# A two-layer expert network on one core: four products of each up-projection burst share one PSUM bank, with three additions in place of five

## The chip, the cores and the metric

The kernel runs on one core of a Trainium2 chip. The metric is the time of one execution in device microseconds; before the change it is 1911.4 us, the median of three runs (1910.29 to 1911.5). The core has five engines that run beside one another and wait for one another by semaphores: TensorE (PE in the profile, its weight loads PEld), VectorE (DVE), ScalarE (ACT), GpSimd (POOL) and SyncE (SP), which here only issues transfers. Each engine takes its instructions in the order in which they stand in its own program.

## The reference

Three parts follow one another. A linear attention over 4 batches of 576 rows gives 2304 rows of 512 numbers. A mixture of 8 experts, all of them applied to every row and weighted by a probability that a Sinkhorn iteration makes, follows; then a feed-forward layer.

```python
h = np.maximum(x @ w1[e], 0.0)            # 2304x512 @ 512x1024, for each e of 8
out += P[:, e:e + 1] * (h @ w2[e])        # 2304x1024 @ 1024x512
...
h = x @ w_in                              # 2304x512 @ 512x2048
g = h * np.clip(h + 3.0, 0.0, 6.0) / 6.0
return g @ w_out
```

## The kernel before

Inputs are float32. Each operand of a large product is split into a float16 high part and a float16 rest, and a product is three matmuls: high by high, high by rest, rest by high.

The up-projection (`x @ w1`) goes by Winograd's form of Strassen's scheme: rows and columns are cut into halves, and seven products of quarter size take the place of eight. For that, seven operands of x lie ready in `xbuf` (QB11, QB21, QB22, QT4, QT1, QT2, QT3 in this order, made by `combine_steps` or `forms`), and seven of a weight slice in `w1buf` (QA11, QA12, QS4, QA22, QS1, QS2, QS3, made by `w1_steps`). The index in `prod(bank, i, first, last)` picks the pair.

The work is cut into 20 slices of 512 hidden columns (`s`, 16 for the experts, 4 for the feed-forward layer) and three pairs of row groups (`p`). `step(s, p, prev)` calls `up_burst` twice, each on a quarter of the slice (`qf` 0 and 1). A burst has seven products of six matmuls of 384 columns (L905), which land in four PSUM banks A, B, C and D of the pool `ps_u`. Two products that belong to one sum are accumulated into one bank by TensorE; the other sums are made by `add` (L913) on VectorE, which reads a bank, scales it and adds an SBUF tile. ScalarE copies bank A out twice (L944 and L951). `emit` then makes the two float16 parts of a hidden tile `h` from a finished sum: ScalarE applies the activation (L933, L937, in the feed-forward layer L927) and the cast (L934, L929), VectorE or GpSimd forms the rest (L935, L938, L930), and in the feed-forward layer VectorE also does L928.

Between the products stand three down-projection tiles of the step before (`down_tile`, L978: twelve matmuls of 512 columns into one of two banks `y`), which VectorE adds onto `acc` (L988). `between[0]` to `between[2]` are these three calls.

All other work is cut into small steps that wait in queues: `tick()`, called at the end of each product and twice in each down tile, takes the next one from `ticks`, `side` or `back`. In `side` lie the scaling and splitting of the next weights (L207 on ScalarE, L208 on VectorE, L269 on GpSimd); in `back` the conversion of the float64 weights of the last layer (L324 to L345, of which L345 is ScalarE's); in `ticks` the rest of the attention, the gate, and the making of the feed-forward layer's x (`x2_steps`, L1022 and L1023, then L377, L378, L382).

There are 60 steps. Steps 6 to 44 and 50 to 59 stand under `tc.manual_schedule()`: there each engine's order is that of the code. The first six steps, and steps 45 to 49, in which the last expert slices and the first feed-forward slice meet `x2_steps`, are ordered by the scheduler of the framework. In the first two of these (s 0 and the p 1 step of s 0) there are no down tiles between the products.

Of the kernel before, what the change touches and what calls it, by code (L numbers as in the profile page):

```python
# [9 lines left out]
F32 = mybir.dt.float32  # L10
# [3 lines left out]
AF = mybir.ActivationFunctionType  # L14
ALU = mybir.AluOpType
# [16 lines left out]
QB11, QB21, QB22, QT4, QT1, QT2, QT3 = range(7)  # L32
# [3 lines left out]
H_DOWN = 2.0 ** -20  # L36
# [4 lines left out]
def tile_attention_moe_ffn(  # L41
# [12 lines left out]
    nc = tc.nc  # L54
    B, H, S, D = q.shape
    NT, DM = out.shape
    E, _, F = w1.shape
    P = 128
# [4 lines left out]
    GN = GJ * P  # L63
# [13 lines left out]
    ps_u = ctx.enter_context(tc.tile_pool(name="ps_u", bufs=1, space=bass.MemoryType.PSUM))  # L77
# [24 lines left out]
    def rt(name):  # L102
        return rpool.tile([P, GN], F32, tag="r", name=name)
# [264 lines left out]
    def combine_steps(p, cp, bs):  # L368


        b11, b21, b12, b22, t1, t2 = bs
        dst = xop[p]
        V, G = nc.vector, nc.gpsimd

        def sp(qd, src, eng):
            def f():
                nc.scalar.copy(dst[:, qd, 0, cp], src)  # L377
                eng.tensor_sub(dst[:, qd, 1, cp], src, dst[:, qd, 0, cp])  # L378
            return f

        def tt(o, a, b):
            return lambda: V.tensor_sub(o, a, b)  # L382

        return [
            tt(t1, b12, b11),
            lambda: (tt(t2, b22, t1)(), sp(QB11, b11, V)()),
            lambda: (sp(QT2, t2, G)(), tt(b12, b22, b12)()),
            lambda: (sp(QT1, t1, V)(), sp(QB21, b21, G)()),
            lambda: (tt(t1, t2, b21)(), sp(QT3, b12, V)()),
            lambda: (sp(QT4, t1, V)(), sp(QB22, b22, G)()),  # L390
        ]

# [9 lines left out]
    def attention(pr):  # L402
# [207 lines left out]
        def forms(p, cp, bank):  # L610

            ga, gb = PAIRS[p]
            dst = xop[p]
            ps = {}

            def out_(ps_, qd):
                nc.scalar.copy(dst[:, qd, 0, cp], ps_)
                nc.vector.tensor_tensor(out=dst[:, qd, 1, cp], in0=ps_, in1=dst[:, qd, 0, cp], op=ALU.subtract)

            def onto(ps_, qds):  # L620
                for m, qd in qds:
                    for hl in range(2):
                        nc.tensor.matmul(
                            ps_, m, dst[:, qd, hl, cp], start=False, stop=True, skip_group_check=True
                        )

            def plain(c, g, qd):
                def f():
                    ps[qd] = bank(f"f{p}_{cp}_{qd}")
                    xset(ps[qd], c, g)  # L630
                    out_(ps[qd], qd)
                return f

            def f_t1():
                b = bank(f"f{p}_{cp}_t1")
                xset(b, cp, gb)
                onto(b, [(minus, QB11)])
                out_(b, QT1)

            def f_on(qd, qds):  # L640
                def f():
                    onto(ps[QB22], qds)
                    out_(ps[QB22], qd)
                return f

            return [
                plain(cp, ga, QB11), f_t1, plain(cp + 2, gb, QB22), f_on(QT2, [(minus, QT1)]),
                plain(cp + 2, ga, QB21), f_on(QT4, [(minus, QB21)]), f_on(QT3, [(plus, QB21), (minus, QB11)]),
            ]
# [17 lines left out]
        a, gap, b = across_max(lambda: t["am"], f"kv{pr}", st)  # L667
# [221 lines left out]
        return zi  # L889


    def up_burst(s, p, qf, hs, between):


        w = w1op[s % 2]
        x = xop[p]
        nm = f"{s}_{p}_{qf}"
        bank = {b: ps_u.tile([P, 512], F32, tag=b, name=f"{b}{nm}")[:, :GN] for b in "ABCD"}
        fs = slice(qf * P, (qf + 1) * P)

        def prod(b, i, first, last):
            n = 0
            for c in range(2):
                for wi, xi in ((0, 0), (0, 1), (1, 0)):
                    nc.tensor.matmul(  # L905
                        bank[b], w[:, i, wi, c, fs], x[:, i, xi, c, :],
                        start=(first and n == 0), stop=(last and n == 5), skip_group_check=True,
                    )
                    n += 1
            tick()  # L910

        def add(o, b, i1, sign=1.0):
            nc.vector.scalar_tensor_tensor(  # L913
                out=o, in0=bank[b], scalar=sign * H_DOWN, in1=i1, op0=ALU.mult, op1=ALU.add
            )

        ffn = s >= NE
        if ffn:
            zi = ffn_zi(s, p)

        def emit(c, grp, fc, clean=False, pool=False):
            h = hpool.tile([P, 2, GN], F16, tag=f"h{grp}", name=f"h{grp}{s}_{p}_{fc}", bufs=(6, 8)[grp])
            hs[grp][fc] = h
            eng = nc.gpsimd if pool else nc.vector
            if ffn:
                r = rt(f"g{grp}{s}_{p}_{fc}")
                nc.scalar.activation(r, c, AF.Relu, scale=zi, bias=three)  # L927
                nc.vector.scalar_tensor_tensor(out=r, in0=r, scalar=6.0 * KAPPA, in1=c, op0=ALU.min, op1=ALU.mult)  # L928
                nc.scalar.copy(h[:, 0, :], r)  # L929
                eng.tensor_sub(h[:, 1, :], r, h[:, 0, :])  # L930
            elif pool:
                if not clean:
                    nc.scalar.activation(c, c, AF.Relu)  # L933
                nc.scalar.copy(h[:, 0, :], c)  # L934
                eng.tensor_sub(h[:, 1, :], c, h[:, 0, :])  # L935
            else:
                nc.scalar.activation(h[:, 0, :], c, AF.Relu)  # L937
                nc.vector.scalar_tensor_tensor(  # L938
                    out=h[:, 1, :], in0=c, scalar=0.0, in1=h[:, 0, :], op0=ALU.max, op1=ALU.subtract
                )  # L940

        r1, r2, r3 = rt(f"r1_{nm}"), rt(f"r2_{nm}"), rt(f"r3_{nm}")
        prod("A", 0, True, False)
        nc.scalar.activation(r1, bank["A"], AF.Copy, scale=H_DOWN)  # L944
        prod("B", 5, True, False)
        add(r2, "B", r1)
        prod("C", 4, True, False)
        prod("D", 3, True, True)
        prod("A", 1, False, True)
        r4 = rt(f"r4_{nm}")  # L950
        nc.scalar.activation(r4, bank["A"], AF.Copy if ffn else AF.Relu, scale=H_DOWN)  # L951
        prod("B", 6, False, True)
        add(r1, "B", r1)
        add(r3, "C", r1)
        add(r1, "D", r1, -1.0)
        emit(r4, 0, qf, clean=True, pool=True)
        between[0]()
        prod("C", 2, False, True)
        emit(r3, 1, qf + 2)
        emit(r1, 0, qf + 2, pool=True)  # L960
        add(r2, "C", r2)
        between[1]()
        emit(r2, 1, qf, pool=True)
        between[2]()

# [68 lines left out]
    with tc.manual_schedule():  # L1034
# [7 lines left out]
        t0, t1 = attention(0), attention(1)  # L1042
# [227 lines left out]
```

## Time and profile before

| | |
|---|---|
| median of three runs | 1911.4 us |
| the profiled execution | 1909.97 us |
| its span, first to last instruction | 1908.2 us |
| mean granted TensorE clock | 0.992 of full speed |
| busy: PE, DVE, ACT, POOL | 1851.7, 1310.4, 774.6, 616.7 us |

The span is the time from the first to the last instruction; 1.8 us of the profiled execution lie outside it. A busy time is the time in which the engine had at least one instruction in work; for PE the ends are modelled. An idle stretch is put down to the instruction whose semaphore came last. What takes the metric is the engine that never rests, and for the others, the moments at which it had to wait for them.

### The profile page before, as it was taken

To read this page: it belongs to the slowest core of one execution; us is meant where nothing else is said; L and a number is where in the kernel's file an instruction comes from. 1 tells how busy PE (TensorE), PEld (TensorE's weight loads), DVE (VectorE), ACT (ScalarE), POOL (GpSimd) and SP (SyncE) were. 2 spreads that over 40 slices of the span, in tenths; PEclk is the share of its full clock that TensorE was granted. 3 is DMA by queue.
4 is the path that set the end of the run, shared out by engine and by line. 5 is a ranking of instruction groups with operands and counts; after the bars stand their busy time and mean duration, and the time that the engine had idled before them with its cause. 6 is when DMAs were issued, how large, how long until landed. Compare 5 with 4: busy or idle time off the path is not lost.

```text
span 1908.2 us, 26933 instructions
## 1 busy us (share of the span) xinstructions
PE 1851.7 (97%) x10642; PEld 987.1 (52%) x10642; DVE 1310.4 (69%) x2325; ACT 774.6 (41%) x1436; POOL 616.7 (32%) x582
## 2 busy tenths in 40 slices
PE   4999999999999999999999999999999999999999
PEld 3555555555555555555555555555555554555554
DVE  8985747676766767575766666676747796667554
ACT  3754434333333334243434333333424355535432
POOL 4342234333332333233333333333322333313121
PEclk7999999999999999999999999999999999999999
DMA  9200001111111111102011111111000100000001
GB/s 293 94 24 1 9 15 56 40 39 56 56 56 40 60 56 39 56 23 72 23 56 47 48 56 61 51 44 56 23 29 1 45 23 23 23 23 22 1 28 72
DMA packets 48430, 87.72 MB, mean 46 GB/s; under 512 B 12208, under 2 KB 12208, under 8 KB 48304
## 3 DMA queue, kind: packets, MB, share of 16 engines
q1 hardware_dynamic: 48304, 86.01, 13.6%
q8 instruction: 83, 1.36, 0.3%
q14 instruction: 43, 0.35, 0.1%
HBM read 72.89 MB, written 13.11 MB: 45 GB/s over the span
## 4 chain that ended last, share of the span: by engine, by line
PE 80%; DVE 13%; ACT 2%; DMA 2%; issue 1%; POOL 1%; SPq 0%; DVEq 0%; POOLq 0%; ACTq 0%
PE y L978 41%; PE C L905 11%; PE B L905 11%; PE A L905 11%; PE D L905 5%; DVE r L913 2%; DVE w1buf L208 2%; DVE g L928 1%; DMA raw<-in_moe_w_dram 1%; DVE w2buf L208 1%; DVE scr L382 1%; DVE acc L555 1%; DVE acc L988 1%; DVE xbuf L378 1%; DVE scr L1023 1%
## 5 line engine op out<-in xcount | busy, mean ns | idle before, releaser
L978 PE MATMUL y<-w2buf,h 128*128 128x512 f16 x4320 | 979.0, 379 | 0.1
L905 PEld LDWEIGHTS <-w1buf 128*128 128x128 f16 x5040 | 491.9, 98 | 366.6 <-issue 21.7
L978 PEld LDWEIGHTS <-h 128*128 128x128 f16 x4320 | 422.6, 98 | 474.1 <-issue 2.3
L935 POOL TENSOR_TENSOR h<-r,h 128x384 f16<-128x384 f32 x288 | 276.4, 960 | 847.2 <-ACT h L934 776.0
L913 DVE SCALAR_TENSOR_TENSOR r<-B,r 128x384 f32<-128x384 f32 x240 | 133.2, 555 | 251.6 <-PE B L905 244.1
L988 DVE SCALAR_TENSOR_TENSOR acc<-y,cf,acc 128x512 f32<-128x512 f32 x252 | 188.5, 748 | 157.2 <-PE y L978 157.0
L905 PE MATMUL B<-xbuf,w1buf 128*128 128x384 f16 x1440 | 274.4, 326 | 6.8 <-DVE r L913 3.4
L905 PE MATMUL C<-xbuf,w1buf 128*128 128x384 f16 x1440 | 274.5, 326 | 5.4 <-DVE r L913 5.4
L905 PE MATMUL A<-xbuf,w1buf 128*128 128x384 f16 x1440 | 275.0, 326 | 1.0 <-ACT r L944 1.0
L951 ACT ACTIVATE r<-A 128x384 f32<-128x384 f32 x120 | 58.8, 490 | 333.9 <-PE A L905 333.9
L933 ACT ACTIVATE r<-r 128x384 f32<-128x384 f32 x192 | 100.3, 522 | 162.2 <-DVE r L913 155.7
L934 ACT CAST h<-r 128x384 f16<-128x384 f32 x288 | 147.4, 512 | 8.4
L930 POOL TENSOR_TENSOR h<-g,h 128x384 f16<-128x384 f32 x72 | 67.7, 940 | 255.1 <-ACT h L929 204.4
L944 ACT ACTIVATE r<-A 128x384 f32<-128x384 f32 x120 | 58.6, 489 | 211.5 <-PE A L905 211.5
L913 DVE SCALAR_TENSOR_TENSOR r<-C,r 128x384 f32<-128x384 f32 x240 | 132.7, 553 | 11.7 <-PE C L905 1.9
L905 PE MATMUL D<-xbuf,w1buf 128*128 128x384 f16 x720 | 137.9, 326 | 1.9 <-DVE xbuf L378 1.1
L929 ACT CAST h<-g 128x384 f16<-128x384 f32 x96 | 49.2, 512 | 96.8 <-DVE g L928 96.8
L937 ACT ACTIVATE h<-r 128x384 f16<-128x384 f32 x96 | 50.2, 523 | 93.6 <-DVE r L913 93.6
L938 DVE SCALAR_TENSOR_TENSOR h<-r,h 128x384 f16<-128x384 f32 x96 | 80.3, 837 | 2.4 <-ACT h L937 2.4
L928 DVE SCALAR_TENSOR_TENSOR g<-g,r 128x384 f32<-128x384 f32 x96 | 62.4, 651 | 13.0 <-ACT g L927 10.4
L927 ACT ACTIVATE g<-r,three,zi 128x384 f32<-128x384 f32 x96 | 67.7, 705 | 7.6 <-DVE r L913 3.2
L913 DVE SCALAR_TENSOR_TENSOR r<-D,r 128x384 f32<-128x384 f32 x120 | 66.8, 556 | 3.8
(621 smaller groups left out, 1487.1 us busy)
## 6 DMA issues: line engine op xcount, KB each, us to landing
raw<-in_moe_w_dram SPq DMA_DIRECT2D x31, 1024.0 KB, 5.8
scr<-in_moe_w_in_dram SPq DMA_DIRECT2D x16, 512.0 KB, 4.2
scr<-in_moe_w_out_dram SPq DMA_DIRECT2D x16, 512.0 KB, 3.6
acc<-in_q_dram SPq DMA_DIRECT2D x4, 1152.0 KB, 8.4
out_dram<-acc SPq DMA_DIRECT2D x18, 256.0 KB, 2.0
win<-scr SPq DMA_DIRECT2D x16, 256.0 KB, 3.3
wout<-scr SPq DMA_DIRECT2D x16, 256.0 KB, 2.2
raw<-win SPq DMA_DIRECT2D x4, 1024.0 KB, 5.2
```

The source lines that it names most:

```text
L905: nc.tensor.matmul(bank[b], w[:, i, wi, c, fs], x[:, i, xi, c, :], start=(first and n == 0), stop=(last and n == 5), skip_group_check=True,)
L913: nc.vector.scalar_tensor_tensor(out=o, in0=bank[b], scalar=sign * H_DOWN, in1=i1, op0=ALU.mult, op1=ALU.add)
L927: nc.scalar.activation(r, c, AF.Relu, scale=zi, bias=three)
L928: nc.vector.scalar_tensor_tensor(out=r, in0=r, scalar=6.0 * KAPPA, in1=c, op0=ALU.min, op1=ALU.mult)
L930: eng.tensor_sub(h[:, 1, :], r, h[:, 0, :])
L933: nc.scalar.activation(c, c, AF.Relu)
L934: nc.scalar.copy(h[:, 0, :], c)
L935: eng.tensor_sub(h[:, 1, :], c, h[:, 0, :])
L938: nc.vector.scalar_tensor_tensor(out=h[:, 1, :], in0=c, scalar=0.0, in1=h[:, 0, :], op0=ALU.max, op1=ALU.subtract)
L951: nc.scalar.activation(r4, bank["A"], AF.Copy if ffn else AF.Relu, scale=H_DOWN)
L978: nc.tensor.matmul(ps, hs[grp][fc][:, hi, ts_], w[:, wi, fc, :], start=(n == 0), stop=(n == 11))
L988: nc.vector.scalar_tensor_tensor(out=acc[:, j, :], in0=ps, scalar=cf, in1=acc[:, j, :], op0=ALU.mult, op1=ALU.add)
```

## The change

The burst keeps its seven products, in another order and in other banks. One bank, now called X, takes products 0, 5, 6 and 3 one onto the other, and ScalarE copies it out after each of the four (L926 in the new file), so that the partial sums of the scheme appear in it one by one. Y takes products 4 and 2, Z product 1. X alternates between the bank tags A and D from burst to burst, Y is always B, Z always C. VectorE has three additions left: Z onto the first copy, Y onto the third, and, after its second product, Y onto the second. The operand QT4 of x has its sign turned, so that product 3 can be accumulated instead of subtracted; this is done where it is made, in `combine_steps` and in `forms`. The tile that needs no activation pass of its own (`clean`) is now the one from X's last product. The down tiles stand after X's second and third products and after Y's second. In the new file the matmuls of the burst are L915, the additions L923, the down tile's matmuls L988 and its addition L998, the passes of `emit` L938 to L949.

```diff
-            lambda: (tt(t1, t2, b21)(), sp(QT3, b12, V)()),
+            lambda: (tt(t1, b21, t2)(), sp(QT3, b12, V)()),
...
             def out_(ps_, qd):
+                if qd == QT4:
+                    nc.scalar.activation(dst[:, qd, 0, cp], ps_, AF.Copy, scale=-1.0)
+                    nc.vector.scalar_tensor_tensor(
+                        out=dst[:, qd, 1, cp], in0=ps_, scalar=-1.0, in1=dst[:, qd, 0, cp], op0=ALU.mult, op1=ALU.subtract
+                    )
+                    return
...
-        bank = {b: ps_u.tile([P, 512], F32, tag=b, name=f"{b}{nm}")[:, :GN] for b in "ABCD"}
+        bursts[0] += 1
+        tags = {"X": "AD"[bursts[0] % 2], "Y": "B", "Z": "C"}
+        bank = {b: ps_u.tile([P, 512], F32, tag=g, name=f"{b}{nm}")[:, :GN] for b, g in tags.items()}
...
-        r1, r2, r3 = rt(f"r1_{nm}"), rt(f"r2_{nm}"), rt(f"r3_{nm}")
-        prod("A", 0, True, False)
-        nc.scalar.activation(r1, bank["A"], AF.Copy, scale=H_DOWN)
-        prod("B", 5, True, False)
-        add(r2, "B", r1)
-        prod("C", 4, True, False)
-        prod("D", 3, True, True)
-        prod("A", 1, False, True)
-        r4 = rt(f"r4_{nm}")
-        nc.scalar.activation(r4, bank["A"], AF.Copy if ffn else AF.Relu, scale=H_DOWN)
-        prod("B", 6, False, True)
-        add(r1, "B", r1)
-        add(r3, "C", r1)
-        add(r1, "D", r1, -1.0)
-        emit(r4, 0, qf, clean=True, pool=True)
+        r1, r2, r3, r4 = (rt(f"r{n}_{nm}") for n in range(1, 5))
+        prod("X", 0, True, False)
+        copy(r1, "X")
+        prod("Y", 4, True, False)
+        prod("Z", 1, True, True)
+        prod("X", 5, False, False)
+        add(r1, "Z", r1)
+        copy(r2, "X")
+        emit(r1, 0, qf, pool=True)
         between[0]()
-        prod("C", 2, False, True)
+        prod("X", 6, False, False)
+        copy(r3, "X")
+        add(r3, "Y", r3)
         emit(r3, 1, qf + 2)
-        emit(r1, 0, qf + 2, pool=True)
-        add(r2, "C", r2)
         between[1]()
+        prod("X", 3, False, True)
+        copy(r4, "X", AF.Copy if ffn else AF.Relu)
+        prod("Y", 2, False, True)
+        emit(r4, 0, qf + 2, clean=True, pool=True)
+        add(r2, "Y", r2)
         emit(r2, 1, qf, pool=True)
         between[2]()
```

How the engines' orders move is shown at three places. The first is ScalarE in a burst of the stretch that follows the code (slice 5, pair 0, first burst; `A5_0_0` is the bank, `r1` to `r4` the float32 tiles, `h05_0_0` a hidden tile). Before:

```order
L944 ACTIVATE r1_5_0_0_5205<-A5_0_0_5201 128x384 [waits PE_49]
L951 ACTIVATE r4_5_0_0_5243<-A5_0_0_5201 128x384 [waits PE_49,Pool_49]
L934 CAST h05_0_0_5255<-r4_5_0_0_5243 128x384 [waits Activation_49]
L937 ACTIVATE h15_0_2_5284<-r3_5_0_0_5207 128x384 [waits DVE_49]
L933 ACTIVATE r1_5_0_0_5205<-r1_5_0_0_5205 128x384 [waits DVE_49]
L934 CAST h05_0_2_5287<-r1_5_0_0_5205 128x384 [waits Activation_49]
L933 ACTIVATE r2_5_0_0_5206<-r2_5_0_0_5206 128x384 [waits DVE_49]
L934 CAST h15_0_0_5314<-r2_5_0_0_5206 128x384 [waits Activation_49]
```

The same engine in the same burst, now:

```order
L926 ACTIVATE r1_5_0_0_5174<-X5_0_0_5171 128x384 [waits PE_49,Pool_49]
L926 ACTIVATE r2_5_0_0_5175<-X5_0_0_5171 128x384 [waits PE_49,Pool_49]
L944 ACTIVATE r1_5_0_0_5174<-r1_5_0_0_5174 128x384 [waits DVE_49]
L945 CAST h05_0_0_5206<-r1_5_0_0_5174 128x384 [waits Activation_49]
L926 ACTIVATE r3_5_0_0_5176<-X5_0_0_5171 128x384 [waits PE_49,Pool_49]
L948 ACTIVATE h15_0_2_5237<-r3_5_0_0_5176 128x384 [waits DVE_49]
L926 ACTIVATE r4_5_0_0_5177<-X5_0_0_5171 128x384 [waits PE_49]
L945 CAST h05_0_2_5279<-r4_5_0_0_5177 128x384 [waits Activation_49]
L944 ACTIVATE r2_5_0_0_5175<-r2_5_0_0_5175 128x384 [waits DVE_49]
L945 CAST h15_0_0_5283<-r2_5_0_0_5175 128x384 [waits Activation_49]
```

There are two copies more, and passes that wait for VectorE now stand between the copies that free X.

The second place is TensorE in the first two bursts of slice 0, which the scheduler orders and which have no down tiles (one row stands for each run of matmuls into a bank; the third number of a name is the burst). Before:

```order
L905 MATMUL A0_0_0_576<-xbuf_83,w1buf0_84 128x384 [waits DVE_49]
...
L905 MATMUL B0_0_0_577<-xbuf_83,w1buf0_84 128x384 [waits DVE_49]
...
L905 MATMUL A0_0_0_576<-xbuf_83,w1buf0_84 128x384 [waits Activation_49]
...
L905 MATMUL B0_0_0_577<-xbuf_83,w1buf0_84 128x384 [waits DVE_49]
...
L905 MATMUL A0_0_1_680<-xbuf_83,w1buf0_84 128x384 [waits Activation_49]
```

The same place on TensorE now:

```order
L915 MATMUL X0_0_0_576<-xbuf_83,w1buf0_84 128x384
L915 LDWEIGHTS w1buf0_84
L915 MATMUL X0_0_1_679<-xbuf_83,w1buf0_84 128x384
...
L915 MATMUL X0_0_0_576<-xbuf_83,w1buf0_84 128x384 [waits Activation_49]
...
L915 MATMUL X0_0_1_679<-xbuf_83,w1buf0_84 128x384
...
L915 MATMUL Z0_0_1_681<-xbuf_83,w1buf0_84 128x384 [waits DVE_49]
...
L915 MATMUL X0_0_0_576<-xbuf_83,w1buf0_84 128x384 [waits Activation_49]
...
L915 MATMUL Y0_0_0_577<-xbuf_83,w1buf0_84 128x384 [waits DVE_49]
```

Products of the second burst now fill the time in which the first burst's X is copied; four matmuls stand in the first such place, and two of X and two of Z in the second.

The third place is VectorE in the second burst of slice 16, pair 0, within steps 45 to 49. Before, from the burst's second addition on:

```order
L913 SCALAR_TENSOR_TENSOR r1_16_0_1_13948<-B16_0_1_13943,r1_16_0_1_13948 128x384 [waits DVE_49]
L208 SCALAR_TENSOR_TENSOR w1buf1_85<-wtmp_89,ws_a17__13897,w1buf1_85 128x512
L913 SCALAR_TENSOR_TENSOR r3_16_0_1_13950<-C16_0_1_13944,r1_16_0_1_13948 128x384 [waits DVE_49,Pool_49]
L1023 TENSOR_SCALAR scr_90<-x2T3_4_14043,sx_95 128x384 [waits PE_49,Pool_49]
L913 SCALAR_TENSOR_TENSOR r1_16_0_1_13948<-D16_0_1_13945,r1_16_0_1_13948 128x384 [waits DVE_49]
L928 SCALAR_TENSOR_TENSOR g016_0_1_14031<-g016_0_1_14031,r4_16_0_1_14012 128x384 [waits Activation_49]
L988 SCALAR_TENSOR_TENSOR acc_91<-y15_15_14036,cf15_12923,acc_91 128x512 [waits PE_49]
```

The same engine, from the same burst's first addition to its second, now:

```order
L923 SCALAR_TENSOR_TENSOR r1_16_0_1_13850<-Z16_0_1_13847,r1_16_0_1_13850 128x384 [waits PE_49]
...
L939 SCALAR_TENSOR_TENSOR g016_0_1_13904<-g016_0_1_13904,r1_16_0_1_13850 128x384 [waits Activation_49]
...
L998 SCALAR_TENSOR_TENSOR acc_91<-y15_15_13909,cf15_12833,acc_91 128x512 [waits PE_49]
L1033 TENSOR_SCALAR scr_90<-x2T1_4_13930,sx_95 128x384 [waits PE_49]
L1033 TENSOR_SCALAR scr_90<-x2T3_4_13943,sx_95 128x384 [waits PE_49,Pool_49]
L208 SCALAR_TENSOR_TENSOR w1buf1_85<-wtmp_89,ws_a17__13793,w1buf1_85 128x512
L923 SCALAR_TENSOR_TENSOR r3_16_0_1_13852<-Y16_0_1_13846,r3_16_0_1_13852 128x384 [waits Activation_49,Pool_49]
```

Three additions that stood close together, each waiting for the one before, have become two that lie a down tile apart.

## Rows read from the trace of the kernel before

**Rows 1.** The page: span, and busy time of each engine.
```profile
span 1908.2 us, 26933 instructions
...
PE 1851.7 (97%) x10642; PEld 987.1 (52%) x10642; DVE 1310.4 (69%) x2325; ACT 774.6 (41%) x1436; POOL 616.7 (32%) x582
```
**Rows 2.** Busy time by stretch: from:to, length, PE, PEld, DVE, ACT, POOL, granted clock.
```profile
50.00:300.00 250.00, 237.47 (x1778) 132.98 (x1775) 172.60 (x353) 125.16 (x238) 75.70 (x80) 0.99 0.09 32
300.00:1440.00 1140.00, 1138.32 (x6102) 598.80 (x6101) 768.35 (x1302) 422.98 (x796) 397.21 (x357) 1.00 0.14 47
1440.00:1530.00 90.00, 87.19 (x483) 48.09 (x482) 72.16 (x131) 37.75 (x74) 28.58 (x28) 1.00 0.07 24
1530.00:1600.00 70.00, 63.49 (x341) 34.26 (x340) 67.33 (x121) 41.79 (x79) 26.96 (x24) 0.98 0.09 31
1540.00:1550.00 10.00, 7.90 (x37) 3.98 (x36) 10.00 (x17) 5.21 (x10) 3.19 (x4) 0.83 0.01 2
1600.00:1850.00 250.00, 248.10 (x1325) 129.82 (x1324) 157.82 (x291) 114.27 (x202) 59.41 (x59) 1.00 0.05 17
```
**Rows 3.** Waits of PE, 50 to 300 us: total us, times, longest.
```profile
PE B L905 <- POOL xbuf L378: 2.2, 2, 1.2
PE C L905 <- DVE r L913: 2.2, 1, 2.2
```
**Rows 4.** Waits of PE, the whole span.
```profile
PE C L905 <- DVE r L913: 5.4, 6, 2.2
```
**Rows 5.** Waits of PE, 1440 to 1600 us.
```profile
PE B L905 <- DVE r L913: 3.1, 2, 1.6
...
PE D L905 <- DVE xbuf L378: 1.1, 2, 0.8
...
PE A L905 <- ACT r L944: 1.0, 1, 1.0
PE D L905 <- ACT xbuf L377: 0.8, 2, 0.5
PE C L905 <- DVE r L913: 0.6, 1, 0.6
```
**Rows 6.** Waits of PE, 1600 to 1908 us.
```profile
PE C L905 <- DVE r L913: 1.3, 2, 0.9
PE B L905 <- DVE r L913: 0.4, 1, 0.4
```
**Rows 7.** The page's groups: line, operation, count, busy us, mean ns; idle before.
```profile
L913 DVE SCALAR_TENSOR_TENSOR r<-B,r 128x384 f32<-128x384 f32 x240 | 133.2, 555 | 251.6 <-PE B L905 244.1
...
L951 ACT ACTIVATE r<-A 128x384 f32<-128x384 f32 x120 | 58.8, 490 | 333.9 <-PE A L905 333.9
...
L944 ACT ACTIVATE r<-A 128x384 f32<-128x384 f32 x120 | 58.6, 489 | 211.5 <-PE A L905 211.5
```
**Rows 8.** The chain of waits, in order of time: start, us, what (one burst).
```profile
601.57 0.97 PE A L905 x6
...
607.42 2.59 PE y L978 x12
```
**Rows 9.** Timeline: a first copy of bank A that was not delayed.
```profile
660.01 1.14 PE L905 MATMUL A<-xbuf,w1buf 128*128 128x384 f16 x6
...
661.18 0.49 ACT L944 ACTIVATE r<-A 128x384 f32<-128x384 f32 x1 [2.48 <-PE A L905]
```
**Rows 10.** Timeline: delayed first copies of bank A.
```profile
1573.14 1.14 PE L905 MATMUL A<-xbuf,w1buf 128*128 128x384 f16 x6
...
1578.75 0.47 ACT L944 ACTIVATE r<-A 128x384 f32<-128x384 f32 x1
...
1757.03 1.14 PE L905 MATMUL A<-xbuf,w1buf 128*128 128x384 f16 x6
...
1759.77 0.47 ACT L944 ACTIVATE r<-A 128x384 f32<-128x384 f32 x1
```
**Rows 11.** The groups by line: ScalarE's pass in the conversion of weights.
```profile
L345 ACT ACTIVATE scr<-scr 128x512 f32<-128x512 int32 x32 | 21.6, 675 | 61.6 <-DVE scr L342 61.3
```

More of the change, by code (lines that the diff above doesn't have):

```diff
@@ L889, in ffn_zi @@
         return zi
+    bursts = [0]
     def up_burst(s, p, qf, hs, between):
@@ L910, in prod, with add, copy @@
             tick()
[L912 to L915, printed above, removed]
+        def add(o, b, i1):
+            nc.vector.scalar_tensor_tensor(out=o, in0=bank[b], scalar=H_DOWN, in1=i1, op0=ALU.mult, op1=ALU.add)
+        def copy(o, b, fn=AF.Copy):
+            nc.scalar.activation(o, bank[b], fn, scale=H_DOWN)
         ffn = s >= NE
```

## The prediction

> **What bounds the kernel now.** I read the page's busy times first. TensorE is at work in 1851.7 of 1908.2 us, VectorE in 1310.4, ScalarE in 774.6 [rows 1]. The change leaves every matmul in place, so it can only remove or add TensorE's idle time. The second view, busy time by stretch, says where that lies [rows 2]: from 300 to 1440 us TensorE rests 1.7 us out of 1140, from 1600 to 1850 us 1.9 out of 250. It rests 12.5 us between 50 and 300 us, 2.8 between 1440 and 1530, and 6.5 in the 70 us after that. The first 50 us hold no burst. What the change can win at most is the sum, 25.4 us.
>
> The third view, what TensorE waited for, gives names to these rests. Behind the bursts' own additions (L913) it waited 2.2 us early [rows 3], 3.1 + 0.6 us between 1440 and 1600 us [rows 5] and 1.3 + 0.4 us in the feed-forward part [rows 6]; of 5.4 us for bank C in the whole span [rows 4] that leaves 5.4 - 2.2 - 0.6 - 1.3 = 1.3 us for the long middle. From 1530 to 1600 us VectorE was busy for 67.33 of 70 us [rows 2]: there VectorE sets the pace, and TensorE waits for its additions and for the making of the next x. In the 10 us from 1540 TensorE's granted clock was 0.83, so a piece of it ran at the half level of 1.2 GHz: 17% of 10 us, or 1.7 us of full-speed work, was lost beside the idle time.
>
> **The change part by part.** There are 120 bursts. VectorE loses two additions in each, 2 x 0.555 us [rows 7] = 1.11 us, in all 133 us. ScalarE gains two copies of the kind of L944 and L951, 2 x 0.49 us [rows 7] = 0.98 us, in all 118 us. As the engine is off TensorE's path, neither sum is time by itself. The turned sign of QT4 swaps the operands of a subtraction or puts a scale on a copy that is made anyway; I put it at nothing: VectorE works there before the first bursts on four tiles, and if the scaled form took as much longer as the addition exceeds the copy (0.555 - 0.489 us), it would be 0.07 us twice in the first phase. No transfer is issued earlier or later in the code.
>
> What counts is how long each bank may be held. A product takes 0.97 us, a down tile 2.59 us [rows 8]. An undelayed copy starts 1.17 us after the first matmul of its product and takes 0.49 us [rows 9], so it is done 1.66 us after that start.
> - X's second product (index 5) comes two products behind its first, 2.92 us after its start: the copy may be 2.92 - 1.66 = 1.26 us late, a little less the semaphore. This is the narrowest cushion of the new burst.
> - The third and the fourth one come 0.97 + 2.59 = 3.56 us after their predecessor's start, a cushion of 1.9 us.
> - Y's second product waits for an addition (0.56 us) behind the third copy; it has 0.97 us more than the fourth product of X, so the cushion is 1.9 + 0.97 - 0.6 = 2.3 us. The next burst's Y is freed by the last addition, with a down tile and a product, 3.56 us, between: 2.7 us.
>
> Before, C's second product needed two additions in a row within one down tile: 2.59 - 0.2 - 2 x 0.56 = 1.27 us. So the narrowest cushion has the same width, but moves from VectorE (67% busy in the long middle, 768 of 1140 us) to ScalarE (37%, 423 of 1140 us [rows 2]). The queue behind it matters as well: ahead of the first copy stand, on ScalarE, the passes of the burst before that wait for VectorE's last addition, and any split or conversion that a tick puts there; behind the copy stand the other copies and all of `emit`, which the next step's down tiles read.
>
> Stage by stage, with this:
> - 50 to 300 us. The wait of 2.2 us for an addition should go. So may some of the 2.2 us for GpSimd's L378 [rows 3], whose operand QT2 was needed second and is now needed fourth; but B21, also GpSimd's, is now needed third, so I count none. In the bursts without down tiles X's products follow one another closely. A matmul follows each 0.97 / 6 = 0.162 us [rows 8], so X is free 0.90 us after the start of its last one (1.17 - 5 x 0.162 + 0.49 + about 0.05, [rows 9]), so four foreign matmuls (4 x 0.162 us, plus its own slot) leave 0.1 us open. The order has five such places, with four matmuls or fewer: at least 0.8 us in all, and 3.8 us if each finds ScalarE (125 of 250 us busy) at the start of another 0.6 us pass. I take 1.7. Stage: -2.2 + 1.7 = -0.5 us, bounds -4.4 to +3.8.
> - 300 to 1440 and 1600 to 1850 us. The additions' waits, 1.3 + 1.7 us, go mostly: -2.1. One new wait is plain in the order: in slice 10, pair 2, the first copy stands behind L345, which waits for three VectorE operations that themselves wait for the down tile just ended. L345 waits 61.6 / 32, or some 2 us, each time already [rows 11], and takes 0.68 us; I take 1.0 us beyond the cushion, for one place. Late copies of the old kind: L944 started more than 1.56 us behind the end of its product's issue 12 times out of 120; six of these lie in these stretches, their excess over the new cushion summing to 3.7 us. With VectorE's load lower, I take 1.5. Stage: +0.4 us, bounds -3.0 to +6.
> - 1440 to 1600 us. 70 us at the slowest are 4.8 bursts of 14.6 us; VectorE is relieved by 4.8 x 1.11 = 5.3 us in a stretch where it is full and TensorE rests 6.5 us. If all of it reached TensorE, 5.3 us would go, and the half-clock piece, 1.7 us, with it; if ScalarE (41.79 of 70 us busy) took over, with 4.7 us more work, nothing would. TensorE's waits for product D's operand (1.1 + 0.8 us [rows 5]) lie with QT4, now needed sixth, but B21 takes its place, so they do not count. I take the middle: -2.6 - 0.9, and +0.3 for one late copy: -3.2 us, bounds -7.0 to +2.
> - The end: the last down tiles need the hidden tile from X's fourth copy. Behind that copy lie four passes, about 3.5 us, against product, down tile and nine matmuls, over 5 us: nothing.
>
> Sum: -0.5 + 0.4 - 3.2 = -3.3 us. The profiled execution, 1909.97 us, becomes 1906.7; the median of the runs lies 1.4 us above it, so 1911.4 - 3.3 = **1908.1 us**.
>
> A rule of the Trainium skill speaks against the change: its page "Perfetto Trace Analysis", section "Optimizing Tensor Performance", Matmuls, says that independent groups of matmuls should go round the PSUM banks, so that reading one out overlaps the next one's matmuls. Here three of seven products follow a read of their own bank. By the rule alone, with nothing between, each would expose 0.74 us (0.90 less its own slot), 3 x 120 x 0.74 = 266 us. The spacing of 1.95 to 2.59 us of other matmuls [rows 8] argues that the overlap is kept by other banks, wherever the copy starts on time; what is left of the rule is the second rival.
>
> **The rivals.**
> - VectorE's relief arrives whole. For it: VectorE at 67.33 of 70 us [rows 2]. Against: the scheduler and the ticks can set other work into the room. Third stage -7.0 us, the others as above: -7.1 us, 1904.3 us.
> - Slower: X's second product waits for a late ScalarE. It is the mechanism above, decided where the first copy is over 1.26 us late. Of the 120 old copies 94 found ScalarE idle and 26 did not; twelve were later than that, the worst starting at 1578.75 for a product begun at 1573.14, the last one at 1759.77 [rows 10]. At the old lateness the excess sums to 12 us; with 0.98 us of copies on top it is some 25 us. The additions' waits that go, 5.4 + 3.1 + 0.4 = 8.9 us, and the 1.0 us of L944 [rows 4 to 6] come off: +2 to +15 us. The middle, +8 us, gives 1919 us. Against it: in the long middle nearly all copies were on time, and lateness came from waiting for VectorE, which now has less to do.
> - The waits only change their names, B21 for T4, ScalarE for VectorE: within 1.9 us, 1911.4 us.
>
> **How the numbers follow.** My forecast has 0.42, with a range of its own of 1905.5 to 1911; the relief 0.20, the late ScalarE 0.16, the exchange 0.22. The range that holds 8 in 10 reaches from 1902 (relief and early gains together) to 1917 (the rival's lower half). A difference under 0.2%, 3.8 us, can't be told from none. Under 1907.6 lie the relief and some 0.4 of my own case: 0.20 + 0.17 = 0.37. Over 1915.2 lies most of the rival: 0.13. That leaves 0.50.
>
> **What would show it.** Busy VectorE down by about 133 us and ScalarE up by about 118 us in the groups. TensorE's idle time from 1530 to 1600 us down from 6.5 us to about 4; "X waits for ScalarE" below 4 us from 50 us on, most of it in the first two steps and in the feed-forward part; no more waits for the additions in the long middle. I am wrong if TensorE waits for L926 by more than about 6 us in all, if the stretch at 1530 us keeps its idle time, or if the middle from 300 to 1440 us grows by over 3 us.

## The result, and the profile after

The changed kernel takes 1923.95 us (median of four runs, 1921.79 to 1926.55) against 1910.85 us for the kernel before: a ratio of 1.0066, with a 95% interval of 1.0055 to 1.0078. It is slower by 13.1 us; 1908.1 was forecast, and the time lies beyond the range. The profiled execution took 1924.41 us, its span is 1922.6 against 1908.2 [rows 1].

The page of the changed kernel, its busy times:

```profile
span 1922.6 us, 26860 instructions
...
PE 1857.6 (97%) x10642; PEld 988.3 (51%) x10642; DVE 1159.9 (60%) x2085; ACT 879.8 (46%) x1676; POOL 609.5 (32%) x582
```

VectorE has lost 150 us (133 forecast) and ScalarE gained 105 (118 forecast), and neither bought time. VectorE's further loss is seen above all in one pass of the expert slices (L938, now L949), whose 96 instructions took 0.58 us each instead of 0.84; why is not shown. ScalarE's copies alone grew by 117 us (480 instead of 240), near the forecast; its busy time counts overlapping instructions once. Busy time by stretch, in the columns of [rows 2]:

```profile
300.00:1440.00 1140.00, 1134.97 (x6083) 597.52 (x6081) 662.55 (x1146) 486.16 (x947) 387.47 (x356) 1.00 0.14 47
...
1530.00:1600.00 70.00, 62.53 (x349) 34.55 (x348) 67.03 (x120) 47.22 (x90) 25.73 (x24) 1.00 0.09 31
1540.00:1550.00 10.00, 7.85 (x47) 4.42 (x45) 10.00 (x16) 6.82 (x14) 2.85 (x4) 1.00 0.01 2
1600.00:1850.00 250.00, 241.07 (x1263) 124.68 (x1262) 130.47 (x246) 128.31 (x228) 56.22 (x56) 0.99 0.04 13
```

From 300 to 1440 us TensorE now rests 1140 - 1134.97 = 5.0 us instead of 1.7 (4.6 of them before 345 us), and from 1600 to 1850 us 8.9 instead of 1.9. What it waits for, over the whole span and in the feed-forward part from 1600 to 1908 us:

```profile
PE X L915 <- ACT r L926: 10.4, 12, 2.1
...
PE csp L828 <- DVE cs L823: 2.9, 1, 2.9
...
PE cm_b__3317 L184 <- DVE wm_b__3302 L245: 2.4, 1, 2.4
...
PE cm_a__3080 L184 <- DVE wm_a__3065 L245: 1.9, 1, 1.9
```

```profile
PE X L915 <- ACT r L926: 7.3, 8, 2.1
PE Y L915 <- DVE r L923: 1.3, 3, 0.6
```

L926 is the copy out of the shared bank. It holds TensorE up for 10.4 us, 7.3 of them in the feed-forward part. The three small matmuls below it are no part of a burst: `csp` belongs to the Sinkhorn iteration, `cm_a` and `cm_b` spread the maximum of a weight that was loaded just before.

To see where the time went I compare, trace by trace, the start of the same instruction: the first matmul of a burst's last down tile (`between[2]`), ahead of which both orders have the same products. How much later than in the kernel before it starts (us; minus is earlier), in all the kernels of this study:

| start in the kernel before | 289.4 | 348.8 | 1435.8 | 1604.9 | 1893.8 | from 1604.9 on |
|---|---|---|---|---|---|---|
| changed kernel | +1.4 | +6.2 | +5.3 | +3.1 | +14.4 | **+11.4** |
| 1: old burst in the feed-forward part | +0.6 | +4.8 | +3.9 | +2.0 | +2.0 | -0.1 |
| 2: no tick ahead of the copy | +1.1 | +8.3 | +7.8 | +5.5 | +10.0 | +4.5 |
| 3: copy ahead of the passes | +0.8 | +5.4 | +4.5 | +2.3 | +4.9 | +2.7 |
| 4: maximum later, slice 2 | -4.0 | +1.6 | +0.6 | -1.6 | +8.0 | +9.7 |
| 5: new burst in the feed-forward part alone | +1.0 | +1.1 | +4.2 | +3.5 | +11.5 | +8.0 |
| 6: both repairs | -4.1 | -4.2 | -5.2 | -7.4 | -4.7 | +2.7 |
| 7: maximum later, slices 2 and 3 | -4.9 | -5.0 | -6.0 | -8.2 | +1.5 | +9.7 |
| 8: kernel before, maximum later | +1.9 | +2.3 | +1.0 | +0.9 | +0.9 | 0.0 |
| 9: old feed-forward burst, maximum later | -3.8 | -3.9 | -4.9 | -6.2 | -6.3 | 0.0 |

The first row is the finding: 1.4 us up to 290 us, 4.8 from there to 349, then -0.9 over 1087 us with 74 of the 120 bursts, -2.2 in the transition, and +11.4 in the feed-forward part. By the same comparison at the down tile of 228.9 us the changed kernel is still 1.7 us ahead, so the early loss lies between 229 and 349 us. Each row is one execution: the changed kernel and experiments 1 to 3 have the same code up to there and stand at +4.8 to +8.3 us at 349 us, so differences of 2 or 3 us between rows are not evidence by themselves. The last column, a difference within one execution, repeats: -0.1 to 0.0 us in the three rows with the old burst there, 2.7 in the two with the copy ahead of the passes.

The largest single loss of that part, in the timeline of the changed kernel (start, us, engine, line, operation; in brackets the wait before it and what ended it):

```profile
1670.99 0.72 ACT L207 ACTIVATE w2buf<-raw,ws_b__15041 128x512 f16<-128x512 f32 x1 [1.59 <-DVE ws_b__15041 L199]
1671.62 0.69 ACT L938 ACTIVATE g<-r,three,zi 128x384 f32<-128x384 f32 x1
...
1672.21 1.14 PE L915 MATMUL X<-xbuf,w1buf 128*128 128x384 f16 x6
...
1673.01 0.51 ACT L940 CAST h<-g 128x384 f16<-128x384 f32 x1 [0.69 <-DVE g L939]
...
1674.96 0.51 ACT L940 CAST h<-g 128x384 f16<-128x384 f32 x1 [0.71 <-DVE g L939]
1675.37 1.94 ACT L207 ACTIVATE w2buf<-raw,ws_b__15041 128x512 f16<-128x512 f32 x3
...
1677.22 0.47 ACT L926 ACTIVATE r<-X 128x384 f32<-128x384 f32 x1
...
1677.74 1.44 PE L915 MATMUL X<-xbuf,w1buf 128*128 128x384 f16 x6 [2.14 <-ACT r L926]
...
1678.98 4.18 PE L988 MATMUL y<-w2buf,h 128*128 128x512 f16 x12
```

The product at 1672.21 was to be copied 1.17 us later [rows 9]; the copy starts 3.84 us late. ScalarE's order puts much ahead of it: a split that waits 1.59 us for the weight's scale, the passes for r4 and r2, each with a round trip through VectorE (0.69 and 0.71 us of waiting), three more splits in a row, and only then the copy. The second product of X waits 2.14 us, and the down tile behind it takes 4.18 us instead of 2.75: a part of it runs at half clock (1.2 GHz), by the granted clock of the 15 us from 1675 (0.89, so 11% of 15 us, 1.7 us, are lost):

```profile
1675.00:1690.00 15.00, 12.86 (x59) 6.05 (x58) 8.04 (x14) 7.56 (x14) 1.82 (x2) 0.89 0.21 70
```

The kernel before has the same three splits ahead of the same copy:

```profile
1667.73 1.14 PE L905 MATMUL A<-xbuf,w1buf 128*128 128x384 f16 x6
...
1668.86 1.94 ACT L207 ACTIVATE w2buf<-raw,ws_b__15153 128x512 f16<-128x512 f32 x3
...
1670.71 0.47 ACT L944 ACTIVATE r<-A 128x384 f32<-128x384 f32 x1
...
1671.63 1.14 PE L905 MATMUL A<-xbuf,w1buf 128*128 128x384 f16 x6
```

There the copy is 1670.71 - 1667.73 - 1.17 = 1.81 us late, and A's second product doesn't wait: three other products stand between the first and it, and its cushion is 3 x 0.97 + 0.97 - 1.66 = 2.2 us. The change made the cushion narrower (1.26 us) and the copy 2.0 us later.

The early loss looks different. VectorE (the maximum, L237 and L245), SyncE (the load) and TensorE (`cm_a`) in the changed kernel:

```profile
293.37 1.14 PE L915 MATMUL X<-xbuf,w1buf 128*128 128x384 f16 x6
...
295.58 1.40 DVE L208 SCALAR_TENSOR_TENSOR w2buf<-raw,ws_b__2940,w2buf 128x512 f16<-128x512 f32 x2
...
297.01 0.37 SPq L263 DMA_DIRECT2D raw<-in_moe_w_dram  x1
...
302.71 1.22 DVE L237 TENSOR_REDUCE am_a__3043<-raw 128x1 f32<-128x1024 f32 x1 [1.90 <-DMA raw<-in_moe_w_dram]
...
305.46 1.21 DVE L237 TENSOR_REDUCE am_a__3043<-raw 128x1 f32<-128x1024 f32 x1
...
307.25 0.15 DVE L245 TENSOR_REDUCE wm_a__3065<-am_a__3043 128x1 f32<-128x2 f32 x1
...
307.45 0.49 PE L184 MATMUL cm_a__3080<-ident,wm_a__3065 128*128 128x128 f32 x2 [1.86 <-DVE wm_a__3065 L245]
```

and the same step in the kernel before:

```profile
291.94 1.14 PE L905 MATMUL A<-xbuf,w1buf 128*128 128x384 f16 x6
...
292.87 1.40 DVE L208 SCALAR_TENSOR_TENSOR w2buf<-raw,ws_b__2957,w2buf 128x512 f16<-128x512 f32 x2
...
294.30 0.37 SPq L263 DMA_DIRECT2D raw<-in_moe_w_dram  x1
...
300.56 1.22 DVE L237 TENSOR_REDUCE am_a__3058<-raw 128x1 f32<-128x1024 f32 x1 [0.75 <-DMA raw<-in_moe_w_dram]
...
303.59 0.15 DVE L245 TENSOR_REDUCE wm_a__3074<-am_a__3058 128x1 f32<-128x2 f32 x1
...
303.95 0.38 PE L184 MATMUL cm_a__3098<-ident,wm_a__3074 128*128 128x128 f32 x2
```

The transfer takes some 6 us in both. Before, TensorE reaches the small matmul 303.95 - 294.30 = 9.65 us after the load's issue, and the maximum is ready; in the changed kernel it stands there 8.6 us after it (307.45 - 1.86 - 297.01), and VectorE has put other work between the two halves of the maximum, so that this is ready 10.4 us after the issue instead of 9.4.

TensorE's own way to this place has not become shorter: from the burst's first product it takes 305.59 - 293.37 = 12.2 us, before 303.95 - 291.94 = 12.0. It is the load that leaves later in the burst, 3.6 us after that product instead of 2.4. In both kernels it leaves within 0.03 us of the end of VectorE's last split of the weight before (L208, ended at 296.98 and 294.27 us), which reads the buffer `raw` that the load overwrites; both traces put SyncE's wait down to that split. The load of 326 us does the same: it leaves 1.0 us behind the start of the burst's first product, and in the kernel before 0.9 us ahead of it.

### The profile page after: what moved, and what is told of

It is laid out like the page before. It is cut to its first block, busy times and chain, and to the rows that moved or that the text cites. A ratio compares the mean times of both kernels' runs of the same rounds, so it can differ in the third digit from the quotient of the medians.

```text
span 1922.6 us, 26860 instructions
## 1 busy us (share of the span) xinstructions
PE 1857.6 (97%) x10642; PEld 988.3 (51%) x10642; DVE 1159.9 (60%) x2085; ACT 879.8 (46%) x1676; POOL 609.5 (32%) x582
## 4 chain that ended last, share of the span: by engine, by line
PE 82%; DVE 12%; ACT 3%; DMA 1%; issue 1%; POOL 0%; SPq 0%; DVEq 0%; ACTq 0%
PE y L988 43%; PE X L915 21%; PE Y L915 11%; PE Z L915 5%; DVE w1buf L208 2%; DVE g L939 1%; DMA raw<-in_moe_w_dram 1%; DVE scr L382 1%; DVE acc L998 1%; DVE r L923 1%; DVE xbuf L378 1%; ACT g L938 1%; DVE w2buf L208 1%; DVE acc L555 1%; ACT w1buf L207 1%
## 5 line engine op out<-in xcount | busy, mean ns | idle before, releaser
L988 PE MATMUL y<-w2buf,h 128*128 128x512 f16 x4320 | 997.2, 380 | 0.0
L915 PEld LDWEIGHTS <-w1buf 128*128 128x128 f16 x5040 | 492.8, 98 | 372.7 <-issue 25.2
L988 PEld LDWEIGHTS <-h 128*128 128x128 f16 x4320 | 422.8, 98 | 468.4 <-issue 5.2
L915 PE MATMUL X<-xbuf,w1buf 128*128 128x384 f16 x2880 | 549.4, 326 | 10.7 <-ACT r L926 10.4
L926 ACT ACTIVATE r<-X 128x384 f32<-128x384 f32 x480 | 234.3, 488 | 596.5 <-PE X L915 587.6
L998 DVE SCALAR_TENSOR_TENSOR acc<-y,cf,acc 128x512 f32<-128x512 f32 x252 | 188.0, 746 | 214.7 <-PE y L988 214.5
L915 PE MATMUL Y<-xbuf,w1buf 128*128 128x384 f16 x1440 | 275.5, 327 | 4.3 <-DVE r L923 3.1
L923 DVE SCALAR_TENSOR_TENSOR r<-Y,r 128x384 f32<-128x384 f32 x240 | 132.5, 552 | 93.6 <-ACT r L926 49.1
L923 DVE SCALAR_TENSOR_TENSOR r<-Z,r 128x384 f32<-128x384 f32 x120 | 66.3, 552 | 121.5 <-PE Z L915 115.7
L915 PE MATMUL Z<-xbuf,w1buf 128*128 128x384 f16 x720 | 138.6, 328 | 0.0
L949 DVE SCALAR_TENSOR_TENSOR h<-r,h 128x384 f16<-128x384 f32 x96 | 55.9, 583 | 52.4 <-ACT h L948 52.4
L938 ACT ACTIVATE g<-r,three,zi 128x384 f32<-128x384 f32 x96 | 67.6, 704 | 28.0 <-DVE r L923 26.8
L348 POOL TENSOR_TENSOR scr<-scr 128x512 f32<-128x512 f32 x32 | 42.4, 1326 | 40.1 <-ACT scr L345 27.5
L998 DVE SCALAR_TENSOR_TENSOR acc<-y,co,acc 128x512 f32<-128x512 f32 x54 | 40.2, 745 | 24.1 <-PE y L988 23.8
L349 POOL TENSOR_TENSOR scr<-scr 128x512 f32<-128x512 f32 x32 | 41.9, 1310 | 2.5
```

Source lines behind the costliest of these rows:

```text
L915: nc.tensor.matmul(bank[b], w[:, i, wi, c, fs], x[:, i, xi, c, :], start=(first and n == 0), stop=(last and n == 5), skip_group_check=True,)
L923: nc.vector.scalar_tensor_tensor(out=o, in0=bank[b], scalar=H_DOWN, in1=i1, op0=ALU.mult, op1=ALU.add)
L926: nc.scalar.activation(o, bank[b], fn, scale=H_DOWN)
L988: nc.tensor.matmul(ps, hs[grp][fc][:, hi, ts_], w[:, wi, fc, :], start=(n == 0), stop=(n == 11))
L998: nc.vector.scalar_tensor_tensor(out=acc[:, j, :], in0=ps, scalar=cf, in1=acc[:, j, :], op0=ALU.mult, op1=ALU.add)
```

## The experiments

Theory A: the loss lies where ScalarE's copy comes too late for X's second product, in the feed-forward part, and in the half clock that follows; the early part is a loss at another place, behind the maximum of the weights. Theory B: a shared bank costs a little in every burst.

**1. The old burst in the feed-forward slices.**

```diff
+        if s >= NE:
+            tags = {b: b for b in "ABCD"}
...
+            prod("A", 0, True, False)      # the burst before the change, with D added
```

> The new burst stays in the expert slices; the feed-forward slices get the old burst of four banks back (QT4 keeps its turned sign, so product D is added there). Theory A (the loss lies at X's second product in the feed-forward part, where ScalarE comes late, and in the half clock behind it): the 11.3 us that the steps from 1600 to 1900 us lost come back, 1924 - 11.3 = 1912.6 us, and TensorE waits for L926 only about 2 us. Theory B (sharing a bank costs a little in every burst): only 24 of 120 bursts change, 24/120 of 13.1 us = 2.6 us, 1921.3 us. Theory C (the half clock comes by itself and not from the wait): the stretches at half clock stay, 2 x 1.5 us of 11.3 remain, about 1916 us.

1914.81 us (ratio to before 1.0019, 1.0009 to 1.0028). TensorE's waits from 1600 to 1900 us:

```profile
PE C L918 <- DVE r L926: 1.3, 2, 0.9
PE B L918 <- DVE r L926: 0.3, 1, 0.3
```

The part costs what it cost before (-0.1 us), and no stretch of it is at half clock. A holds, B falls; so does C, that the half clock comes by itself: it is absent from this part in all five traces of changed kernels without the waits of 2.14 us (experiments 1, 2, 3, 6 and 9). The median lies 2.2 us above A's 1912.6; the profiled execution, from which the row in the table comes, was the fastest of ten (1912.08).

**2. No tick ahead of the first copy.**

```diff
     def tick():
+        if held[0]:
+            return
...
+        held[0] = s > NE
         between[2]()
```

(`held` is taken back right after the first copy.)

> The changed kernel, but in the feed-forward slices after the first no tick is taken between the last down tile of a burst and X's first copy, so no weight split stands on ScalarE ahead of that copy; the steps come later by as many ticks. Theory A1 (the splits are what makes the copy late): the two waits of 2.14 us and the half clock behind them go, about 2 x 4 us, 1916 us. Theory A2 (the passes of the burst before, which wait for VectorE, make it late, the splits only by 1.9 us in a row): the waits of 2.14 shrink to about 0.3 us, the smaller ones (0.4 to 0.9 us) stay, 1917 us. Theory B (a little in every burst): within 1 us of the changed kernel, 1923 to 1925 us.

1920.81 us (1.0051, 1.0037 to 1.0066). The waits from 1600 to 1900 us:

```profile
PE Y L919 <- DVE r L927: 2.1, 3, 1.5
PE X L919 <- ACT r L930: 1.7, 3, 0.9
PE cm_a__15562 L188 <- DVE wm_a__15547 L249: 1.6, 1, 1.6
PE cm_b__15044 L188 <- DVE wm_b__15029 L249: 1.3, 1, 1.3
```

The median lies above both forecasts of theory A (1916 and 1917). Both waits of 2.1 us and the half clock are gone, so the splits are a necessary part of the lateness. But the moved ticks set the small matmuls for the maximum at places where VectorE is late, and 2.9 us of the gain went there; the part still loses 4.5 us. B falls here too; A1 and A2 aren't told apart.

**3. The copy ahead of the passes for r2.**

```diff
         copy(r1, "X")
+        while late:
+            late.pop()()
...
-        emit(r2, 1, qf, pool=True)
+        if s > NE:
+            late.append(lambda: emit(r2, 1, qf, pool=True))
```

(r2 then lies in `scr`, which is free in these slices.)

> The changed kernel, but in the feed-forward slices after the first the passes on a burst's last sum (r2) stand behind the next burst's first copy instead of ahead of it; the ticks stay where they were. Theory A1 (the splits make the copy late): the three splits in a row (1.94 us) still stand ahead of the copy, the two large waits stay at 1 us or more, 1919 to 1922 us. Theory A2 (the passes that wait for VectorE make it late): ScalarE comes to the splits 1.9 us sooner, the large waits fall to about 0.3 us and the smaller ones go, 1914 us. Theory B: within 1 us of the changed kernel.

1915.51 us (1.0029, 1.0019 to 1.0038). The same place as above, in this kernel's timeline:

```profile
1670.56 1.14 PE L915 MATMUL X<-xbuf,w1buf 128*128 128x384 f16 x6
...
1671.77 1.94 ACT L207 ACTIVATE w2buf<-raw,ws_b__15038 128x512 f16<-128x512 f32 x3
...
1673.61 0.47 ACT L926 ACTIVATE r<-X 128x384 f32<-128x384 f32 x1
...
1674.13 1.14 PE L915 MATMUL X<-xbuf,w1buf 128*128 128x384 f16 x6 [0.19 <-ACT r L926]
1675.10 2.75 PE L995 MATMUL y<-w2buf,h 128*128 128x512 f16 x12
```

The three splits still stand ahead of the copy, yet the wait is 0.19 us: A2, as far as one cause can be named. Read with experiment 2, passes and splits make the lateness together (3.84 us), and taking away either brings it near the cushion; here the copy is still 1.88 us late. The smaller waits did not go, as A2 had it. From 1600 to 1900 us:

```profile
PE X L915 <- ACT r L926: 2.7, 4, 1.2
```

2.3 of these 2.7 us are now two waits of X's fourth product, 1.2 and 1.1 us, which were 0.6 each in the changed kernel: the third copy, with r1's passes and splits ahead of it, is 3.25 and 3.12 us late instead of 2.66.

**4. The maximum of the weights three ticks later, for slice 2.**

```diff
-        steps = [load, None, None, None] + w_scale(...)
+        steps = [load] + [None] * (6 if s == 2 else 3) + w_scale(...)
```

> The changed kernel, but for the weights of slice 2 alone the maximum is taken three ticks later after the load is issued (six empty ticks instead of three). Theory A (VectorE reaches the maximum before the weight has landed, stands still for 1.9 and 5.5 us, and TensorE's small matmul for the maximum waits 1.86 and 2.41 us behind it): the stretch from 300 to 345 us gets back 4 to 4.8 us, 1919.5 us, and the waits for cm_a and cm_b fall below 0.5 us. Rival (the transfers are late by themselves and the small matmul would wait three ticks later too, or the later splits delay the next step): no gain, 1923 to 1926 us.

1918.05 us (1.0039, 1.0024 to 1.0053): better than forecast, but not where. I had taken the loads at 297 and 326 us for those of slice 2; they are slice 3's. The edit took effect from 225 us on: the wait of 2.9 us for `csp` and the half clock behind it went (5.5 us against the changed kernel by 289 us), the one for `cm_a` with it, while the last one stayed, with a half clock behind it:

```profile
PE cm_b__3342 L184 <- DVE wm_b__3327 L245: 2.9, 1, 2.9
```

**5. The converse of 1: the new burst in the feed-forward slices alone.**

```diff
+        if s < NE:      # the four-bank burst in the expert slices
```

> The converse of the first experiment: the old burst of four banks in the expert slices (with the turned sign of QT4, product D added), the new burst only in the feed-forward slices. Theory A (the loss lies in the feed-forward part, where the passes and the splits ahead of the first copy make it late): TensorE shows the two waits of 2.1 us for L926 with the half clock behind them as in the changed kernel, and the steps from 1600 us on lose some 11 us; the early waits behind the scale of the weights go back to those of before: about 1921 us. Theory B (a little in every burst): 24 of 120 bursts, 2.6 us over before, 1913.5 us.

1919.48 us (1.0045, 1.0031 to 1.0059). The waits from 1600 to 1900 us are the changed kernel's to the tenth:

```profile
PE X L918 <- ACT r L929: 7.3, 8, 2.1
PE Y L918 <- DVE r L926: 1.3, 3, 0.6
```

The part loses 8.0 us. It is the loss without any half clock: in this execution none followed. B is excluded (1913.5 us), and A's 1921 is 1.5 us off. The early waits are back at those of before; the +4.2 us at 1436 us come from a wait of the old burst at 1286 us, 2.1 us for C with half clock behind it.

**6 and 7. The maximum later for slices 2 and 3: with the repair of experiment 3 (6), and alone (7).** The edit is that of 4 with `s in (2, 3)`.

> The changed kernel with two repairs together: the passes on a burst's last sum behind the next burst's first copy (feed-forward slices after the first), and the maximum of the weights of slices 2 and 3 taken three ticks later. If the two losses stand in different places and add up (theory A): 1915.5 - 5.9 = 1909.6 us, and the wait of 2.9 us for the maximum of slice 3's second weight goes too, with the half clock behind it (1.5 us): 1906 us, faster than before. Rival (the early waits only move, to the next small matmul behind VectorE, as in the fourth experiment, where one of 2.9 us took the place of one of 2.4): 1909 to 1912 us, no faster than before.

> The changed kernel with the later maximum for slices 2 and 3 alone; the feed-forward part as in the changed kernel. Theory A: the waits for csp (2.9), cm_a (1.9) and cm_b (2.4 us) all go, with the half clock at 234 us: 1918 - 4.4 = 1914 us, the two waits for L926 of 2.1 us in the feed-forward part still there. Rival (the early waits only move): 1917 to 1919 us as with slice 2 alone.

Experiment 7: 1912.48 us (1.0011, 1.0002 to 1.0021); from 200 to 345 us TensorE waits for nothing over 0.15 us, and the feed-forward part keeps its waits (9.7 us lost, with one fall to half clock). Experiment 6: **1905.07 us, ratio to before 0.9969 (0.9957 to 0.9980), faster than both kernels.** From the changed kernel the repairs bring 8.4 (experiment 3) and 11.5 us (experiment 7), together 18.9 of 19.9: separate losses that add up. The long middle by stretch:

```profile
300.00:1440.00 1140.00, 1139.62 (x6111) 600.32 (x6110) 662.17 (x1149) 488.82 (x952) 389.34 (x359) 1.00 0.14 47
```

TensorE rests 0.4 us of these 1140.

**8. The kernel before, with the same later maximum.**

> The kernel before with the same later maximum for slices 2 and 3. If the early waits come from the pace of the new burst against the load alone, the kernel before has little to win there (csp 0.8 + 0.8 + 1.5, cm_b 0.3 us): within 2 us of 1910.8. If the place of the weights' steps is a lever of its own, it gains the 3 us of its waits for csp too: 1907 to 1908 us, and what the changed kernel gains by it says nothing on the burst.

1912.34 us (1.0004, 0.9995 to 1.0013): no gain. The waits for `csp` shrink, and one for the old burst's additions takes their place. From 200 to 345 us, first in the kernel before, then in this one:

```profile
PE csp L822 <- DVE cs L817: 2.2, 2, 1.5
```

```profile
PE C L905 <- DVE r L913: 2.4, 1, 2.4
PE csp L822 <- DVE cs L817: 1.7, 2, 1.0
```

A stretch at half clock follows the wait of 2.4 us and is part of the result. From 235 to 245 us VectorE is busy for 8.91 of 10 us, with splits of the weights (L208) ahead of the burst's additions. So the lever brought nothing with the old burst; that only the old burst's additions stood in its way is my reading and is not shown.

**9. The old burst in the feed-forward part, and the later maximum.**

> The new burst in the expert slices, the old burst of four banks in the feed-forward slices, and the maximum of the weights of slices 2 and 3 three ticks later. If the losses stand in separate places and each place keeps its own price: 1905.1 us with both repairs, less the 2.7 us that its feed-forward part still loses against the kernel before, is 1902.4 us. Rival (the transition from 1440 to 1600 us, where the old burst then runs in the first feed-forward slice, gives the 2.2 us gained there back): 1904.5 to 1906 us, no better than both repairs.

1904.72 us (0.9968, 0.9956 to 0.9980), like experiment 6, and 2.3 us above the sum of the places (1902.4). The profiled execution lies 6.3 us ahead of the kernel before at the end, against 4.7 in experiment 6; the medians differ by 0.35 us. The transition gains 1.4 us instead of 2.2; that explains 0.8 of the 2.3 us, the rest stays open.

## Why the prediction was wrong

- **The failing step** is "Late copies of the old kind ... their excess over the new cushion summing to 3.7 us. With VectorE's load lower, I take 1.5." The number of late copies was about right: of 120 first copies 15 start over 1.26 us late, 12 did before. Their size was wrong (for the six old ones I now count 3.4 us, near the 3.7). From 1600 us on six are 1.61, 2.94, 3.84, 1.79, 2.03 and 3.83 us late, an excess of 8.5 us, and TensorE waits 7.3 us for these copies and for X's others. I had taken the old lateness over, but the new code puts the passes for r4 and for r2 both behind X's last product, so twice as many stand ahead of the next first copy. I named that queue and didn't price it.
- **The cushion** was compared with the wrong one. I set X's 1.26 us against C's 1.27 and found "the same width". The copy that moves was the old burst's A with 2.2 us; the trace of before shows a copy 1.81 us late for which A's second product did not wait. That row would have been the one to look for.
- **The half clock** had a term only where before showed one. In the feed-forward part the changed kernel fell to half clock twice; the loss was 11.4 us, against 8.0 in experiment 5 without it.
- **50 to 345 us.** The wait for the old addition went, as forecast. At 229 us the changed kernel is 1.7 us ahead, in line with the -0.5 that were forecast. What follows was in no term: the wait of 2.9 us for `csp` with a stretch at half clock behind it (+1.4 us by 290 us, still inside the bounds), and 4.8 us more by 349 us, where the small matmuls for a maximum stand too near to their load. I had written "No transfer is issued earlier or later in the code", which is true of the code; but the load waits for VectorE's last split of the weight before, and that now ends later in the burst. Why it does was not tested by a run of its own; between the first split and the other three ScalarE lets 3.0 us pass instead of 1.6 (290.39 to 293.37, before 288.66 to 290.24), with the passes of r4 and r2 between them instead of r2's alone, as in the feed-forward part.
- **The long middle was right:** -0.9 us from 349 to 1436 us; the place in slice 10 cost 0.4 us where I put 1.0. The shared bank costs nothing there, with 1.95 to 2.59 us of other matmuls between; in the feed-forward part, where the reader is late, going back to four banks (experiment 1) gave the 11.4 us back. The Trainium skill ("Perfetto Trace Analysis", "Optimizing Tensor Performance") asks that independent groups of matmuls go round the banks, so that reading one out overlaps the next one's matmuls. The traces of the feed-forward part agree with it (11.4 us), those of the long middle show no price (-0.9 us).
- **1440 to 1600 us:** -2.2 us, -3.2 forecast. The 70 us hold four bursts, not the 4.8 that I counted, so VectorE's relief was 4.4 us at most. The half-clock piece went, as counted (1.00 instead of 0.83 from 1540 to 1550 us). But from 1530 to 1600 us VectorE is still busy for 67.03 us and TensorE rests 7.5: the relief did not reach TensorE there.
- **The rival "slower" was the case:** its place, its price (+2 to +15 us, measured +13.1) and its condition (a first copy over 1.26 us late) came true, but for the early losses, which belong to no rival. That the price fits is partly luck: by the table 6.2 us were lost by 349 us, and they were not in its sum. Of my three signs for being wrong all came: L926 holds TensorE up for 10.4 us (6 allowed), the stretch at 1530 us keeps its idle time, and that from 300 to 1440 us rests 3.3 us longer (3 allowed). I gave it 0.16, because in the long middle copies were on time; the feed-forward part, with its passes through VectorE, has another queue, and it decided.

## What to carry to other kernels

A bank that is read and written on has to be judged by the queue ahead of its reader, in the stage with the longest queue, and by the cushion that the same reader had before. Where a change moves the last product of a group, list what its results now put behind it on the reading engine, and move the next group's read ahead of that. Steps that are spaced by ticks behind a load keep their place, but the load itself leaves only when the last reader of its buffer is done: where a change delays that reader, the distance to the step that needs the load shrinks. Count that distance for each load that a wait hangs on.

## What the runs showed of the hardware

The granted clock does not answer to a wait of one length in one way. Of the eight waits of 2.14 us in the feed-forward part (two each in the changed kernel and experiments 4, 5 and 7) four were followed by a stretch at the half level of 1.2 GHz. In experiment 7 the first of them was not:

```profile
1666.47 1.14 PE L915 MATMUL X<-xbuf,w1buf 128*128 128x384 f16 x6 [2.14 <-ACT r L926]
1667.44 2.75 PE L988 MATMUL y<-w2buf,h 128*128 128x512 f16 x12
```

The down tile took 2.75 us, where the same one in the changed kernel took 4.18. The part loses 11.4 us with two such falls, 9.7 with one and 8.0 with none: 1.7 us for each. What decides whether one follows stays open.
